# Three edits to the order of instructions: sums of tokens, first operands of the last stage, outputs of a pair

## The chip, the cores and the metric

The kernel runs on one core of a Trainium2 chip. The metric is the device time of one launch in microseconds (us); a kernel's time is the median of its runs. The engines are named as the profile names them: PE (matrix multiplications), DVE (vector engine), ACT (scalar engine), POOL (GpSimd), SP (SyncE, which issues most of the transfers). Each engine takes its instructions in the order in which they were issued to it.

## The reference

One input x of 2048 tokens by 576 features is normalised, and three things are added up: the input, a Fourier mixing of the normalised tokens, and a two-layer network on them.

```python
xn = layernorm(x)                                  # 2048 x 576
a, b = xn @ dft_hid_re.T, xn @ dft_hid_im.T        # transform along the features
y = dft_seq_re @ a - dft_seq_im @ b                # real part of the transform along the tokens
h = maximum(xn @ w1, 0)                            # 576 -> 4608
out = x + y + h @ w2                               # 4608 -> 576
```

All inputs are float32, and the four transform matrices are inputs like the others.

## The kernel before

**Arithmetic.** A float32 operand is split into two half-precision parts, hi and lo: ACT writes hi (a scaled copy that rounds), and DVE writes lo (the value minus hi). `split` (L182 on ACT, L183 on DVE) is the general form. A product takes three passes on PE: hi by lo, hi by hi, lo by hi. Larger products are cut into 2 by 2 blocks and done with seven block products in place of eight. The price is sums and differences of blocks on DVE and ACT; the names A11, S1 to S4, T1 to T4 and P1 to P7 are those blocks, block sums and products.

**Stages.** The tokens lie in four groups g of 512.

1. Normalisation of the first group, then the network in nine blocks b of 512 hidden units, each for four groups: a step is one pair (b, g). In a step PE computes the hidden values of (b, g) and the second product of the step before (`mlp2`, L510: seven products; evictions on ACT at L519 and on DVE at L521, from block 1 on added to a spill in main memory by POOL's queue). In blocks 0 and 1 the hidden values come from plain products of 512 columns (`mlp1_step`, L310; outputs in `mlp1_out`, L353 to L361, the last two being hi on ACT and lo on DVE of the four sums S1 to S4). While block 0 runs, the tokens of the following groups are still being normalised, and their weights loaded, scaled and split.
2. From block 2 on, the hidden values come from `pair_products` (L440; seven products on half the columns). They need sums of tokens as right-hand operands: `sums_x` makes four per group, 16 in all, with 56 DVE operations (L405, L406, L408, L409 and lo at L414) and 16 copies on ACT (L412). They are stored in the memory in which block 0's accumulators lay, once these have been written out, and use two temporaries in the weight buffers of block 1. They are handed out as small steps from an iterator `tq` between the products of block 1 and, as far as any are left, of block 2.
3. `dft1`: the transform along the features, for 16 tiles t of 128 tokens (PE at L1002). Outputs R[t]: a copy on ACT (L1022), sums on DVE (L1024 to L1027), hi on ACT (L1030) and lo on DVE (L1031) of three blocks, and at the end hi (L1033) and lo (L1034) of the four sums T.
4. The last stage: 16 units, each with seven products of 24 matmuls (L1116) that sum over 8 tiles R. The left-hand operand of each is made from a unit's four loads `c` by `operand` (L1055 to L1071: sums on DVE at L1063, L1064, L1066 and L1068 where the product needs them, then `split`) into a ring `cs` of four buffers, three products ahead. Evictions are on DVE (L1122). The first three operands are made before the stage begins: their steps come from a list `todo`, one step after each tile of `dft1` from t = 2 on. Ahead of the three stand the scale of the operands, the loads of the first unit, and empty steps, so that the three are called after tiles 13, 14 and 15.

**What sets the order.** The program's calls are only a draft. A planner with its own estimates of times sorts the instructions, and may move one ahead of others on its engine where no dependence forbids it. `tc.issue_after(ins)` forbids it: what is issued inside it stays behind `ins` if it is on the same engine; no wait is added. `order["s"]` is the latest hi of the four sums on ACT (L360, and L459 in `pair_products`), `order["lo"]` the latest lo on DVE (L361, L462).

**A pair's list.** In a step of block 2 and after, two `pair_products` (`first`, `second`) are woven with the step's seven second products (`m`), with small steps of the weights' preparation (`ready`), with passes over the transform matrices (`count`), and with the hi and lo of the sums (`end`). `first(q)` issues a product with what frees its bank; `later1(q)` and `later2(q)` issue what makes outputs of it. The order is a list of pairs (L919 to L927 of the kernel before).

Of the kernel before, what the change touches and what calls it, by code (L numbers as in the profile page):

```python
# [13 lines left out]
AF = mybir.ActivationFunctionType  # L14
ALU = mybir.AluOpType
# [34 lines left out]
def kernel(  # L50
# [17 lines left out]
    nc = tc.nc  # L68
# [119 lines left out]
    means, factors, shifts, order = {}, {}, {}, {}  # L188
# [190 lines left out]
    def halves(g, q):  # L379

        r, c = q
        k, t = 2 * r, (H1, H2)[c]
        return xT[g][:, k : k + 2, t], xT[g][:, KM + 1 + k : KM + 3 + k, t]
# [7 lines left out]
    def sums_x(g):  # L391


        f = [
            w[:, 2 * KT * P :][:, : 2 * GH].rearrange("p (k t) -> p k t", t=GH) for w in w1bufs[2:]
        ]
        tt = nc.vector.tensor_tensor
        for q, (head, tail) in enumerate((
            ((0, 1), (0, 0)), ((1, 1), None), ((1, 0), None), ((1, 1), (0, 1)),
        )):  # L400
            t = f[q % 2]
            h, l = halves(g, head)
            if tail:
                h2, l2 = halves(g, tail)
                tt(t, h, h2, ALU.subtract)  # L405
                tt(t, t, l2, ALU.subtract)  # L406
            else:
                tt(t, h, f[1 - q % 2], ALU.subtract)  # L408
            tt(t, t, l, ALU.add)  # L409
            yield  # L410
            hi, lo = (xsums[g][:, q, n] for n in range(2))
            nc.scalar.activation(hi, t, AF.Copy)  # L412
            yield
            tt(lo, t, hi, ALU.subtract)  # L414

    banks1, ends = [], []

# [464 lines left out]
    for n in range(2, len(steps)):  # L882
        b, g = steps[n]
        pb, pg = steps[n - 1]
        if g == 0 and b:
            if b + 1 < NB:
                todo += prepare_block(b + 1)
            else:
                todo += [lambda: (load_d(0), load_d(1)), lambda: None, new_d, lambda: None]
                for j in range(4):  # L890
                    d = power_d(j)
                    todo += [lambda d=d: next(d), lambda d=d, j=j: (later(d), split_d(j))]
                    if j < 2:
                        todo += [lambda j=j: load_d(j + 2), lambda: None]
                todo += [scales_d]
        if b == 0 and g + 1 < NG:
            with tc.issue_after(order["lo"]):
                weave(stats([(g + 1) * TG + i for i in range(TG)]))
        if b == NB - 1 and g:

            size = 2 * EH
            if g == 1:
                w = mlp.tile([P, 2, 7, EH], F16, tag="w2s", name="sums", bufs=4)
                w = [w.rearrange("p n q e -> p (n q e)").bitcast(F32)]
            elif g == 2:
                w = [raw.tile([P, KT, EH], F32, tag="raw", name=f"sums{k}") for k in range(2)]
                w = [r.rearrange("p k e -> p (k e)") for r in w]
            sumbufs[:] = [
                r[:, k : k + size].rearrange("p (c e) -> p c e", e=EH)
                for r in w for k in range(0, r.shape[1] - size + 1, size)  # L910
            ]
        if b >= BB:
            first, second = (pair_products(b, g, i) for i in range(NQ))
            later1, later2 = (lambda q, f=f: f(q, True) for f in (first, second))
            m = lambda q: mlp2(pb, pg, q)
            end = lambda q: ends and ends.pop(0)()
            ready = lambda q: [work() for _ in range(q)]
            count = lambda q: n > 3 and passes and passes.pop(0)()
            for do, q in (  # L919
                (first, P1), (first, P2), (m, 0), (end, 0), (first, P6), (ready, 1),  # L920
                (first, P5), (later1, P2), (ready, 1), (m, 1), (end, 0), (second, P1), (ready, 1),
                (first, P7), (m, 2), (second, P2), (later1, P7), (ready, 1),
                (first, P3), (first, P4), (count, 0), (later1, P3), (m, 3), (later1, P4), (second, P6),
                (later2, P2), (ready, 1), (m, 4), (end, 0), (second, P5), (ready, 1), (m, 5), (end, 0),
                (second, P7), (ready, 1), (m, 6), (ready, 2), (second, P3), (later2, P7),
                (count, 0), (second, P4), (later2, P3), (later2, P4), (ready, 1),
            ):  # L927
                do(q)
            for _ in range(4):
                next(tq, None)  # L930
            continue
        ps = []
        for i in range(NF):
            if n == 2:
                ps.append(early.pop(0) if early else mlp1(b, g, i))
            else:
                mlp1_step(b, g, i, ps)
            if i % 2:
                mlp1_out(b, g, i // 2, *ps[i - 1 : i + 1])
            if b == 0 and g + 1 < NG:  # L940
                t = (g + 1) * TG + i
                normalize(t)
                remainder(t, nc.gpsimd)
                transposes(t)
            if n == 2 and i == 2:
                todo += prepare_block(1)
            for _ in range(1 if b else 3):
                work()
            for q in range(2 * i, min(2 * i + 2, 7)):
                mlp2(pb, pg, q)  # L950
                if b:
                    next(tq, None)
            if b and i == 3:
                next(tq, None)
            for _ in range(1 + i % 2 if b else 3):
                work()
            if n > 3 and i % 2 and passes:
                passes.pop(0)()
# [30 lines left out]
    def dft1(t):  # L989
# [40 lines left out]
            nc.scalar.activation(hi, src, AF.Copy, scale=r)  # L1030
            stt(lo, src, r, hi, ALU.mult, ALU.subtract)  # L1031
        hi, lo = (R[t][:, n, T3 : T2 + 1] for n in range(2))
        nc.scalar.activation(hi, T, AF.Copy)  # L1033
        nc.vector.tensor_tensor(lo, T, hi, ALU.subtract)  # L1034

    A = {}

# [18 lines left out]
    def operand(m):  # L1056

        n, i = divmod(m, 7)
        q = PRODUCTS[i][0]
        a11, a22, a12, a21 = (A[n, j] for j in range(4))  # L1060
        tt = nc.vector.tensor_tensor
        if q == S2:
            tt(a21, a21, a22, ALU.add)  # L1063
            tt(a11, a21, a11, ALU.subtract)  # L1064
        elif q == S3:
            tt(a21, a22, a11, ALU.subtract)  # L1066
        elif q == S4:
            tt(a12, a12, a11, ALU.subtract)  # L1068
        src = {A11: a11, A22: a22, A12: a12, S1: a21, S2: a11, S3: a21, S4: a12}[q]
        w = csp[m] = cs.tile([P, 2, HK, P], F16, tag="cs", name=f"cs{m}")  # L1070
        split(w[:, 0], w[:, 1], src, sc["c"][:, n : n + 1])  # L1071

    todo += [power_c, lambda: None, lambda: load_c(0)] + [lambda: None] * 8
    todo += [lambda m=m: operand(m) for m in range(3)]
    for t in range(NT):
        if t and t % TG == 0:
            xpool[t // TG - 1].release()
# [104 lines left out]
```

## Time and profile before

| what | value |
|---|---|
| median of 3 runs | 1283.66 us (1282.51 to 1285.61) |
| the profiled execution | 1285.6 us, of which its span is 1283.8 |
| PE busy | 1247.0 us, 97% of the span |
| DVE busy | 1002.9 us, 78% |
| ACT busy | 727.8 us, 57% |
| POOL busy | 149.0 us, 12% |
| moved | 150.75 MB |

Times in the profile count from the start of the span. A row of a timeline gives the start, the length, the engine, the line, the operation, output<-inputs with their shapes, the number of instructions drawn together, and in brackets the idle time of the engine ahead of it and what ended that. A group has the count, busy time, mean of one in ns, and the idle time ahead of its members with the releasers. Matmuls overlap, so a row of n matmuls lasts a little longer than n times their distance.

Block 0 ends near 138 us (the last lo of its hidden values), block 1 runs to about 217, where PE's first L440 matmuls stand between those of L510, and block 2's first pair has its lo at 233. `dft1` runs from 830, where its first matmuls stand between the last of L510, to 949, and the last stage from there to the end.

### The profile page before, as it was taken

How to read it: one execution, taken by the hardware profiler on the slowest of the kernel's cores; microseconds unless marked ns; L12 is line 12 of the kernel's file. 1: busy time of each engine (PE TensorE's matmuls, PEld its weight loads, DVE VectorE, ACT ScalarE, POOL GpSimd, SP SyncE). 2: the span in 40 equal slices, each digit the busy share in tenths (PEclk: the TensorE clock that was granted, in tenths of full speed). 3: DMA queues.
4: the chain of work that ended last, by engine and by line, in shares of the span. 5: the costliest groups of instructions: out<-in, count | busy, mean ns of one | idle time of the engine just before them, and what ended most of it. 6: DMA issues, size and time to landing. Idle time of an engine off the chain costs nothing.

```text
span 1283.8 us, 25483 instructions
## 1 busy us (share of the span) xinstructions
PE 1247.0 (97%) x10396; PEld 990.4 (77%) x10396; DVE 1002.9 (78%) x1879; ACT 727.8 (57%) x1218; POOL 149.0 (12%) x188
## 2 busy tenths in 40 slices
PE   7899999999999999999999999999999999999998
PEld 7665566888888888878878887867777777777776
DVE  8989998786877776777867877567668788888875
ACT  5835567676776676766766765544443333333332
POOL 2320012111112121211121111100000000000000
PEclk9899999999999999999999999999999999999999
DMA  6112457566756675666666665630033435344320
GB/s 242 43 62 69 124 124 153 131 116 142 146 131 122 133 149 121 133 136 126 120 142 143 138 135 121 111 94 17 1 124 113 153 105 165 117 127 135 127 85 20
DMA packets 60806, 150.75 MB, mean 117 GB/s; under 512 B 6288, under 2 KB 21136, under 8 KB 60688
## 3 DMA queue, kind: packets, MB, share of 16 engines
q1 hardware_dynamic: 42256, 111.36, 27.1%
q0 software_dynamic: 18432, 37.76, 20.9%
q8 instruction: 81, 1.33, 0.4%
q14 instruction: 37, 0.30, 0.1%
HBM read 101.91 MB, written 47.19 MB: 116 GB/s over the span
## 4 chain that ended last, share of the span: by engine, by line
PE 69%; DVE 17%; ACT 5%; DMA 5%; issue 3%; SPq 1%; POOL 0%; ACTq 0%; POOLq 0%; DVEq 0%
PE p L1116 25%; PE p L510 17%; PE bank L440 17%; PE pd L1002 7%; DMA raw_w<-in_w_dram 2%; DVE w2s L183 2%; PE p L310 2%; ACT h L459 1%; DVE h L448 1%; DVE h L462 1%; ACT f L874 1%; DMA c<-in_cim_dram 1%; DMA c<-in_cre_dram 1%; DVE dbuf L183 1%; DVE w1buf L183 1%
## 5 line engine op out<-in xcount | busy, mean ns | idle before, releaser
L510 PE MATMUL p<-w2s,h 128*128 128x288 f16 x3024 | 409.8, 286 | 4.7 <-DVE acc L521 2.0
L510 PEld LDWEIGHTS <-h 128*128 128x128 f16 x3024 | 295.0, 98 | 81.3 <-issue 6.1
L1116 PE MATMUL p<-R,cs 128*128 128x288 f16 x2688 | 329.6, 286 | 1.8 <-DVE o L1122 1.8
L1116 PEld LDWEIGHTS <-cs 128*128 128x128 f16 x2688 | 263.0, 98 | 68.2 <-issue 2.0
L182 ACT ACTIVATE cs<-c,sc_c 128x1024 f16<-128x1024 f32 x112 | 128.5, 1148 | 205.1 <-PE p L1116 151.3
L183 DVE SCALAR_TENSOR_TENSOR cs<-c,sc_c,cs 128x1024 f16<-128x1024 f32 x112 | 143.7, 1283 | 50.9 <-ACT cs L182 50.8
L440 PEld LDWEIGHTS <-w1buf 128*128 128x128 f16 x1600 | 156.4, 98 | 30.4 <-issue 9.3
L440 PEld LDWEIGHTS <-dbuf 128*128 128x128 f16 x1200 | 117.3, 98 | 22.7 <-issue 7.0
L440 PE MATMUL bank<-xT,w1buf 128*128 128x256 f16 x832 | 109.8, 273 | 1.9 <-ACT acc L469 1.9
L1002 PE MATMUL pd<-dbuf,xT 128*128 128x288 f16 x832 | 106.0, 289 | 2.4 <-DVE R L1031 2.4
L440 PE MATMUL bank<-acc,w1buf 128*128 128x256 f16 x768 | 102.1, 272 | 4.6 <-DVE acc L470 2.9
L462 DVE TENSOR_TENSOR h<-s,h 128x1024 f16<-128x1024 f32 x56 | 68.5, 1224 | 48.4 <-ACT h L459 48.4
L1002 PEld LDWEIGHTS <-xT 128*128 128x128 f16 x832 | 81.5, 99 | 25.8 <-issue 4.8
L523 POOL DMA_DIRECT2D spill<-dbuf x74 | 64.1, 868 | 291.9 <-DVE dbuf L521 225.8
L440 PE MATMUL bank<-xT,dbuf 128*128 128x256 f16 x624 | 82.3, 273 | 1.6 <-ACT acc L469 1.6
L447 ACT ACTIVATE h<-acc 128x256 f16<-128x256 f32 x112 | 46.3, 414 | 59.9 <-DVE acc L470 43.6
L440 PE MATMUL bank<-acc,dbuf 128*128 128x256 f16 x576 | 76.6, 272 | 3.1 <-ACT s L468 1.7
L448 DVE SCALAR_TENSOR_TENSOR h<-acc,h 128x256 f16<-128x256 f32 x112 | 47.3, 423 | 35.1 <-ACT h L447 34.8
L1122 DVE SCALAR_TENSOR_TENSOR o<-p,us_c,o 128x288 f32<-128x288 f32 x112 | 57.5, 514 | 20.3 <-PE p L1116 20.3
L459 ACT ACTIVATE h<-s 128x1024 f16<-128x1024 f32 x56 | 59.0, 1053 | 20.9 <-DVE s L454 19.6
L874 ACT ACTIVATE f<-f 128x1024 f32<-128x1024 f32 x64 | 67.1, 1049 | 5.1 <-DMA f<-in_cre_dram 5.1
L519 ACT ACTIVATE dbuf<-p,c_ub 128x576 f32<-128x576 f32 x74 | 54.1, 732 | 21.4 <-ACT h L447 11.3
(158 smaller groups left out, 1538.7 us busy)
## 6 DMA issues: line engine op xcount, KB each, us to landing
spill<-dbuf POOLq DMA_DIRECT2D x74, 288.0 KB, 5.2
f<-in_cre_dram SPq DMA_DIRECT2D x32, 512.0 KB, 4.5
f<-in_cim_dram SPq DMA_DIRECT2D x32, 512.0 KB, 3.7
c<-in_cre_dram SPq DMA_DIRECT2D x32, 512.0 KB, 4.6
c<-in_cim_dram SPq DMA_DIRECT2D x32, 512.0 KB, 4.8
spill<-sum POOLq DMA_DIRECT2D x38, 288.0 KB, 5.2
raw_w<-in_w_dram SPq DMA_DIRECT2D x17, 640.0 KB, 5.0
raw_w<-in_w_dram SPq DMA_DIRECT2D x18, 576.0 KB, 3.8
```

What stands on the lines that cost most here:

```text
L182: nc.scalar.activation(hi, src, AF.Copy, scale=s)
L183: nc.vector.scalar_tensor_tensor(lo, src, s, hi, ALU.mult, ALU.subtract)
L440: nc.tensor.matmul(ps, l, r, start=first and m == 0, stop=m == len(todo) - 1, skip_group_check=not first,)
L448: stt(lo, src, 0.0, hi, ALU.max, ALU.subtract)
L459: order["s"] = nc.scalar.activation(hi_s, st[:, 1:], AF.Copy).ins
L462: order["lo"] = nc.vector.tensor_tensor(lo_s, st[:, 1:], hi_s, ALU.subtract).ins
L510: nc.tensor.matmul(ps[:, c], h[:, x, qa, c * P : (c + 1) * P], w[:, y, qb], start=first and i == 0 and j == 0, stop=i == NQ - 1 and j == 2 ...
L523: nc.gpsimd.dma_start(spill[g, row, col], o, accum_op=ALU.add)
L874: nc.scalar.activation(f, f, AF.Abs, scale=2.0**-10, accum_out=sums_c[:, n, q : q + 1])
L1002: nc.tensor.matmul(ps[j], xT[g][:, kx, c * P : (c + 1) * P], dsp[j][:, hl, k], start=(t % 2 == 0 and n == 0), stop=(t % 2 == 1 and n == le ...
L1116: nc.tensor.matmul(ps, w[:, a, k], r[:, c, rq], start=first and k == 0 and j == 0, stop=k == HK - 1 and j == 2, skip_group_check=not first,)
L1122: nc.vector.scalar_tensor_tensor(o, ps, us["c"][:, n : n + 1], o, ALU.mult, ALU.add)
```

## The change

1. In `sums_x`, the DVE operations are issued behind `order["lo"]` and the copy behind `order["s"]`, as they are at the moment of the call: behind the latest hidden values' lo and hi.
2. In `dft1`, `order["lo"]` and `order["s"]` are set to the lo and hi of T, and the first three operands of the last stage are issued behind them on DVE and ACT. The three calls come after tiles 13, 14 and 15.
3. In the list of a pair's step, the outputs of P7, P3 and P4 of the first product, some of the sums' hi and lo, and the outputs of P7 of the second, come later.

```diff
@@ -400,18 +400,21 @@
         )):
             t = f[q % 2]
             h, l = halves(g, head)
-            if tail:
-                h2, l2 = halves(g, tail)
-                tt(t, h, h2, ALU.subtract)
-                tt(t, t, l2, ALU.subtract)
-            else:
-                tt(t, h, f[1 - q % 2], ALU.subtract)
-            tt(t, t, l, ALU.add)
+            with tc.issue_after(order["lo"]):
+                if tail:
+                    h2, l2 = halves(g, tail)
+                    tt(t, h, h2, ALU.subtract)
+                    tt(t, t, l2, ALU.subtract)
+                else:
+                    tt(t, h, f[1 - q % 2], ALU.subtract)
+                tt(t, t, l, ALU.add)
             yield
             hi, lo = (xsums[g][:, q, n] for n in range(2))
-            nc.scalar.activation(hi, t, AF.Copy)
+            with tc.issue_after(order["s"]):
+                nc.scalar.activation(hi, t, AF.Copy)
             yield
-            tt(lo, t, hi, ALU.subtract)
+            with tc.issue_after(order["lo"]):
+                tt(lo, t, hi, ALU.subtract)
 
     banks1, ends = [], []
 
@@ -919,11 +922,11 @@
             for do, q in (
                 (first, P1), (first, P2), (m, 0), (end, 0), (first, P6), (ready, 1),
                 (first, P5), (later1, P2), (ready, 1), (m, 1), (end, 0), (second, P1), (ready, 1),
-                (first, P7), (m, 2), (second, P2), (later1, P7), (ready, 1),
-                (first, P3), (first, P4), (count, 0), (later1, P3), (m, 3), (later1, P4), (second, P6),
-                (later2, P2), (ready, 1), (m, 4), (end, 0), (second, P5), (ready, 1), (m, 5), (end, 0),
-                (second, P7), (ready, 1), (m, 6), (ready, 2), (second, P3), (later2, P7),
-                (count, 0), (second, P4), (later2, P3), (later2, P4), (ready, 1),
+                (first, P7), (m, 2), (second, P2), (ready, 1), (first, P3), (first, P4), (count, 0),
+                (later1, P7), (m, 3), (second, P6), (later1, P3), (later1, P4), (later2, P2),
+                (ready, 1), (m, 4), (second, P5), (ready, 1), (m, 5), (end, 0), (second, P7),
+                (end, 0), (ready, 1), (m, 6), (count, 0), (ready, 2), (second, P3), (second, P4),
+                (later2, P7), (later2, P3), (later2, P4), (ready, 1),
             ):
                 do(q)
             for _ in range(4):
@@ -1030,8 +1033,8 @@
             nc.scalar.activation(hi, src, AF.Copy, scale=r)
             stt(lo, src, r, hi, ALU.mult, ALU.subtract)
         hi, lo = (R[t][:, n, T3 : T2 + 1] for n in range(2))
-        nc.scalar.activation(hi, T, AF.Copy)
-        nc.vector.tensor_tensor(lo, T, hi, ALU.subtract)
+        order["s"] = nc.scalar.activation(hi, T, AF.Copy).ins
+        order["lo"] = nc.vector.tensor_tensor(lo, T, hi, ALU.subtract).ins
 
     A = {}
 
@@ -1071,7 +1074,11 @@
         split(w[:, 0], w[:, 1], src, sc["c"][:, n : n + 1])
 
     todo += [power_c, lambda: None, lambda: load_c(0)] + [lambda: None] * 8
-    todo += [lambda m=m: operand(m) for m in range(3)]
+    def first_operand(m):
+        with tc.issue_after(order["s"]), tc.issue_after(order["lo"]):
+            operand(m)
+
+    todo += [lambda m=m: first_operand(m) for m in range(3)]
     for t in range(NT):
         if t and t % TG == 0:
             xpool[t // TG - 1].release()
```

## The prediction

> **What bounds the kernel now.** I read the page's busy shares and groups first, then the windows by stage, then the idle time in TensorE's (PE's) timeline with its releasers, because PE turns out to be the bound.
>
> ```profile
> span 1283.8 us, 25483 instructions
> PE 1247.0 (97%) x10396; PEld 990.4 (77%) x10396; DVE 1002.9 (78%) x1879; ACT 727.8 (57%) x1218; POOL 149.0 (12%) x188
> L1116 PE MATMUL p<-R,cs 128*128 128x288 f16 x2688 | 329.6, 286 | 1.8 <-DVE o L1122 1.8
> ```
>
> PE is idle for 1283.8 − 1247.0 = 36.8 us in all, and the whole last stage (L1116) holds one wait of 1.8. So a gap that vanishes anywhere earlier shortens the run by its length, and a new one at the last stage's start lengthens it by its length.
>
> ```profile
> core 0: us, PE busy (x) PEld busy (x) DVE busy (x) ACT busy (x) POOL busy (x), PEclk, DMA share, GB/s
> 60.00:138.40 78.40, 72.70 (x486) 43.95 (x484) 69.94 (x142) 36.09 (x59) 7.27 (x9) 1.00 0.26 88
> 138.40:233.30 94.90, 94.12 (x641) 61.38 (x639) 84.52 (x167) 62.33 (x109) 13.70 (x17) 1.00 0.55 122
> ```
>
> Columns: window, length, busy time of each engine. Block 0 (60 to 138.4) holds 5.7 us of PE's idle time while the vector engine (DVE) is 89% busy; block 1 (to 233.3, where block 2's first h is complete) holds 0.8. This is measured on one execution of 1285.6 us (span 1283.8 and 1.8 around it), 1.9 above the median of the runs, 1283.66. I sum changes and apply them to both.
>
> **The pair order (third edit).** It changes the order of calls; a planner decides the order of instructions. In the built kernels, the DVE, PE and scalar engine (ACT) streams of blocks 2 to 7 are the same, instruction by instruction. I cost it at nothing there, with no cover needed. The streams differ in blocks 0 and 1, at one place in block 8, and around the first transform.
>
> **Sums held back, what leaves block 0.** These are the sums that DVE makes there now:
>
> ```profile
> L409 DVE TENSOR_TENSOR dbuf<-dbuf,xT 128x512 f32<-128x512 f32 x5 | 3.9, 784 | 0.0
> L414 DVE TENSOR_TENSOR acc<-dbuf,acc 128x512 f16<-128x512 f32 x5 | 3.4, 679 | 0.7 <-DMA spill<-acc 0.7
> L406 DVE TENSOR_TENSOR dbuf<-dbuf,xT 128x512 f32<-128x512 f32 x3 | 2.3, 754 | 0.0
> L405 DVE TENSOR_TENSOR dbuf<-xT 128x512 f32<-128x512 f16 x3 | 2.1, 709 | 0.3 <-POOL dbuf L250 0.3
> L408 DVE TENSOR_TENSOR dbuf<-xT,dbuf 128x512 f32<-128x512 f16 x2 | 1.4, 692 | 0.9 <-PE pt L263 0.9
> ```
>
> That is 18 operations, 3.9 + 3.4 + 2.3 + 2.1 + 1.4 = 13.1 us. In the built order all 18 and their ACT copies go behind block 0's last h. PE's waits in block 0 that have a sum ahead of their releaser, and one DVE row:
>
> ```profile
> 81.01 3.10 PE L510 MATMUL p<-w2s,h 128*128 128x288 f16 x24 [0.58 <-DVE acc L521]
> 84.72 1.14 PE L510 MATMUL p<-w2s,h 128*128 128x288 f16 x8 [0.62 <-DVE acc L521]
> 100.99 2.97 PE L310 MATMUL p<-xT,w1buf 128*128 128x512 f16 x13 [1.17 <-ACT xT L265]
> 117.00 0.27 PE L158 MATMUL pm<-ident,mb 128*1 128x128 bf16 x2 [0.40 <-DVE mb L614]
> 137.15 0.42 PE L510 MATMUL p<-w2s,h 128*128 128x288 f16 x2 [0.86 <-ACT h L360]
> ```
>
> ```profile
> 83.25 0.69 DVE L414 TENSOR_TENSOR acc<-dbuf,acc 128x512 f16<-128x512 f32 x1 [0.71 <-DMA spill<-acc]
> ```
>
> The rows add to 0.58 + 0.62 + 1.17 + 0.40 + 0.86 = 3.6. The second wait is plain: DVE itself stood 0.71 in a sum's store, which waits until the spilled accumulator has been written out, with PE's eviction (L521) behind it. The others are queueing: the xT copy waits on ACT behind a weight split whose scale DVE makes late. The last two can have a weight load beneath them and may stay, and buffers freed earlier may only let PE reach the next load sooner: I take −3.4, between −1.2 (the two evictions alone) and −5.3 (nearly all of the 5.7).
>
> **What they cost in block 1.** DVE has to fit them in by block 2:
>
> ```profile
> 140.00:200.00 60.00, 60.00 (x384) 36.37 (x383) 59.45 (x118) 37.47 (x62) 8.26 (x10) 1.00 0.51 110
> 220.00:233.30 13.30, 13.30 (x118) 11.24 (x116) 6.56 (x15) 8.17 (x19) 0.86 (x1) 1.00 0.54 121
> ```
>
> ```profile
> 177.99 0.81 DVE L521 SCALAR_TENSOR_TENSOR dbuf<-p,c_ub,dbuf 128x576 f32<-128x576 f32 x1
> 180.25 3.10 PE L510 MATMUL p<-w2s,h 128*128 128x288 f16 x24
> 204.81 1.63 PE L510 MATMUL p<-w2s,h 128*128 128x288 f16 x12 [0.78 <-DVE dbuf L521]
> ```
>
> Of 94.9 us DVE is busy 84.5, and adding the 13.1 gives 97.6 (by starts of instructions, which overlap a little at the ends, 82.8 + 12.3 = 95.1). From 140 to 200 DVE idles 0.55 us in 60, so it needs almost no idle time when its queue is full; the slack, 6.7 us, lies after 220. The extra work there therefore starts late by 7 us less the 2.5 to 3 that DVE gains from block 0's gaps. PE does not follow one for one: the eviction at 177.99 ends at 178.8 and its next matmul is the thirteenth of the 24 from 180.25, at 181.6 (2.8 spare), and in the new order 5 to 13 plain matmuls go ahead of the waiting ones (row at 100.99: 2.97 / 13 = 0.22 each, 1.1 to 2.9). But the eviction before 204.81 has no spare, PE already waits 0.78 for it. I take +1.5, from 0 (all covered) to +7.6 (the slower rival). Nothing is gained: PE's idle time here is that 0.78. The sums' ACT copies (16, beside 62 of 94.9 us busy) are covered. The SyncE queue takes one w2 load a place earlier, ahead of a spill, and GpSimd moves one reduction four spills on; both move by single places and no wait on them ends last here: 0.
>
> **Block 8.** One addition (L470) moves ahead of a 1.72 us split:
>
> ```profile
> 781.55 1.72 DVE L183 SCALAR_TENSOR_TENSOR dbuf<-raw_d,c_sd,dbuf 128x1440 f16<-128x1440 f32 x1
> 783.18 0.42 DVE L470 TENSOR_TENSOR acc<-bank,acc 128x256 f32<-128x256 f32 x1
> 783.66 0.82 PE L440 MATMUL bank<-acc,w1buf 128*128 128x256 f16 x6 [1.36 <-DVE acc L470]
> ```
>
> 1.72 is more than the wait: −1.4 (0 if the split then holds up the next eviction, −1.4 at most).
>
> **First operands held back, the start of the first transform.** Now two operand splits sit among the first tiles' evictions and wait for their loads:
>
> ```profile
> 844.40 1.15 ACT L182 ACTIVATE cs<-c,sc_c 128x1024 f16<-128x1024 f32 x1 [5.89 <-DMA c<-in_cre_dram]
> 848.75 1.15 ACT L182 ACTIVATE cs<-c,sc_c 128x1024 f16<-128x1024 f32 x1 [2.81 <-DMA c<-in_cim_dram]
> ```
>
> ```profile
> 850.89 0.28 PE L1002 MATMUL pd<-dbuf,xT 128*128 128x288 f16 x1 [0.45 <-DVE R L1031]
> 851.74 0.28 PE L1002 MATMUL pd<-dbuf,xT 128*128 128x288 f16 x1 [0.57 <-DVE R L1031]
> 853.36 6.86 PE L1002 MATMUL pd<-dbuf,xT 128*128 128x288 f16 x41 [1.34 <-DVE R L1031]
> ```
>
> ```profile
> 851.10:854.50 3.40, 1.49 (x12) 1.01 (x11) 3.40 (x6) 1.94 (x3) 0.00 (x0) 1.00 0.00 0
> 854.50:857.90 3.40, 3.40 (x17) 2.17 (x15) 3.37 (x6) 0.90 (x1) 0.00 (x0) 0.50 0.00 0
> 963.70:967.10 3.40, 1.70 (x14) 1.36 (x14) 3.37 (x4) 1.11 (x1) 0.00 (x0) 1.00 0.42 170
> ```
>
> ACT's evictions of R stand behind a split for 5.89 and 2.81 us, and PE then waits 0.45 + 0.57 + 1.34 = 2.36. After a window in which PE was busy 1.49 of 3.40, the granted clock (eighth column) is 0.50 for one window: another 3.40 × 0.5 = 1.7. After the last row's window, 1.70 of 3.40, it was not (row at 965.40 below: 29.81 / 242 = 0.123 a matmul, full pace). With the splits behind tiles 13 and 14, both costs go: −4.1 (−2.4 to −4.5; the queue then meets only evictions, which keep pace from 860 on).
> The Trainium skill, page "TensorE: Matmul & The Clock Gate", section "HAM oscillation — how this bites in real kernels", gives the rule as "no PE-idle gaps >~3.4µs"; by it these gaps would be free of it. The trace differs: single gaps of at most 1.34 us, 2.36 together, brought a half-clock window.
>
> **The same operands, the start of the last stage.** The third operand (S2) needs two additions and a split, and all three now stand behind R15's last lo (L1034).
>
> ```profile
> 948.76 14.86 PE L1116 MATMUL p<-R,cs 128*128 128x288 f16 x120
> 965.40 29.81 PE L1116 MATMUL p<-R,cs 128*128 128x288 f16 x242 [1.77 <-DVE o L1122]
> ```
>
> ```profile
> 953.15 1.36 DVE L1034 TENSOR_TENSOR R<-T,R 128x1152 f16<-128x1152 f32 x1 [0.30 <-ACT R L1033]
> 963.70 1.23 DVE L1063 TENSOR_TENSOR c<-c,c 128x1024 f32<-128x1024 f32 x1 [3.45 <-DMA c<-in_cre_dram]
> ```
>
> ```profile
> L182 ACT ACTIVATE cs<-c,sc_c 128x1024 f16<-128x1024 f32 x112 | 128.5, 1148 | 205.1 <-PE p L1116 151.3
> L183 DVE SCALAR_TENSOR_TENSOR cs<-c,sc_c,cs 128x1024 f16<-128x1024 f32 x112 | 143.7, 1283 | 50.9 <-ACT cs L182 50.8
> L1122 DVE SCALAR_TENSOR_TENSOR o<-p,us_c,o 128x288 f32<-128x288 f32 x112 | 57.5, 514 | 20.3 <-PE p L1116 20.3
> ```
>
> In before's clock: products 0 and 1 are 48 matmuls from 948.76 at 14.86 / 120 = 0.124, to 954.7. R15's lo lets DVE go at 954.4; L1063 1.2, one eviction 0.4 (0.51 less the overlap of the next), L1064 1.2: 957.2. ACT makes hi in 1.15 to 958.4, DVE lo in 1.28 to 959.7. PE idles 954.7 to 958.4 = 3.8, does two matmuls of product 2 and two of product 3 (whose hi ends near 959.6) in the built order, and waits 0.9 more for lo: +4.7. The gap spans parts of two 3.4 us windows, and one of them will be under half busy in nearly any phase: +1.7. Against that, the wait of 1.77 at 965.40 goes, since DVE's stop for unit 1's loads (3.45) then lies beside PE's new gap, and unit 2's first load, now ahead of eight reloads of outputs on SyncE's queue, moves behind unit 1's: −1.8. Net +4.6, from +2.9 (no slow window) to +6.4 (the 1.77 stays). Queued behind the held additions on DVE are the evictions of products 0 and 1; PE needs their banks only four products on.
>
> **Sum.** −3.4 + 1.5 − 1.4 − 4.1 + 4.6 = −2.8, beside −0.4 of small waits of block 0 (each under 0.25) that go with the sums: −3.2. The profiled execution would take 1285.6 − 3.2 = 1282.4 and the median 1283.66 − 3.2 = 1280.4. A change of 0.2%, 2.57 us, is about what a measurement of this kernel can tell: faster is below 1281.1, slower above 1286.2.
>
> **Rivals.**
> Slower: DVE becomes the bound in block 1. If its 10.4 us of idle time there are waits that come back whatever is queued (in order: for ACT's hi, for a product), all 12.3 us of added work come on top; less the lead of 2.7 and 2.0 of plain matmuls ahead PE gets 7.6 instead of 1.5: −3.2 + 6.1 = +2.9, 1286.6. It decides from 7.3 in block 1. The 0.55 idle in 60 us speaks against it, the eviction without spare at 204.81 for it.
> No change: block 0's waits turn into waits for weights that arrive when they did, and only the two evictions' 1.2 is gained: −3.2 + 2.6 = −0.6, 1283.1. For it: the waits at 117.00 and 137.15 lie next to weight steps. Against: the two evictions and the xT copy have no load of weights beneath them.
> Faster: no slow window at the transition, −3.2 − 1.7 = −4.9, 1278.8; by the row at 963.70 it takes a window half busy, with 3.8 us of gap split evenly over two.
> By the skill's rule above the gap would have to fill a whole 3.4 us window, and 3.8 us seldom does; it would give this same rival's 1278.8.
> That the third edit changes blocks 2 to 7 after all: no, the order there is the same.
>
> **Chances.** The forecast 0.42, from 1278.6 to 1282.4, two thirds of it under 1281.1 (0.27 faster, 0.15 same); the faster rival 0.18; no change 0.20; slower 0.20. Together 0.45, 0.35, 0.20. The range goes from 1276.9 (the faster rival with block 0's gain at 5.3 and the first transform's at 4.5) to 1287.0 (the slower rival and 0.4).
>
> **What the new profile would show.** Block 0: no L405 to L414 before 137, PE's idle time there under 2.5 us, its last h lo some 3 to 4 us earlier. Block 1: DVE near 99% until the first pair of block 2, PE's waits on L521 around 200 to 233 of 1 to 3 us in all; 7 or more proves the slower rival. 783: no wait. 845 to 858: no wait, PEclk 1.00. The last stage: PE waits about 3.8 and 0.9 behind `cs` at product 2, one window at 0.50 after it, and no wait of 1.77. The prediction fails if block 1's overrun passes 7, if block 0's gaps only change their releaser, or if the planner's order runs otherwise because loads land at other times.

## The result and the profile after

The changed kernel takes 1288.01 us (median of 13 runs, 1284.96 to 1290.39) against 1283.69 for the kernel before, run beside it: a ratio of 1.0027, 95% interval 1.0014 to 1.0039. It is slower by about 3.5 us by the ratio (the two medians differ by 4.3), where 1280.4, faster, was forecast; the range ended at 1287.0. The profiled execution took 1289.39 us (span 1287.6), 1.4 above the median.

The page of the changed kernel (its lines stand three to seven below those of the kernel before: L513 was L510, L1123 was L1116):

```profile
span 1287.6 us, 25468 instructions
PE 1247.5 (97%) x10396; PEld 990.2 (77%) x10396; DVE 1003.7 (78%) x1879; ACT 727.5 (56%) x1218; POOL 147.3 (11%) x188
L513 PE MATMUL p<-w2s,h 128*128 128x288 f16 x3024 | 409.9, 286 | 9.2 <-DVE dbuf L524 2.6
L1123 PE MATMUL p<-R,cs 128*128 128x288 f16 x2688 | 332.2, 288 | 4.0 <-ACT cs L182 4.0
```

The work is the same; the second products (L513) wait 9.2 us and not 4.7, and the last stage (L1123) 4.0 and not 1.8. Where the time went is read from PE's order: each kernel issues 10396 matmuls, and the start of the n-th in one profile less its start in the profile of before gives how far PE is ahead or behind at that place. Worked out from the traces (negative is ahead):

| n | place | before, us | changed | sums alone (e1) | 10 moved (e11) | 18 moved (e12) |
|---|---|---|---|---|---|---|
| 1000 | block 0 | 123.1 | −3.2 | −4.7 | −3.6 | −4.2 |
| 1100 | start of block 1 | 140.5 | −3.9 | −5.4 | −4.6 | −4.9 |
| 1550 | end of block 1 | 211.9 | +1.6 | −0.5 | −4.1 | +1.3 |
| 2000 | block 2 | 265.2 | +5.3 | +1.7 | −2.9 | +6.0 |
| 6340 | block 8, before the edit's place | 779.9 | +4.1 | −0.4 | −3.0 | +3.5 |
| 6400 | block 8, after it | 788.2 | +2.6 | −0.4 | −4.5 | +2.0 |
| 7000 | first transform | 863.7 | −1.1 | +0.8 | −8.2 | −1.3 |
| 7780 | start of the last stage | 957.6 | +5.7 | +0.8 | −8.2 | −1.3 |
| 10000 | last stage | 1231.5 | +3.8 | +2.9 | −5.7 | −1.5 |

Such columns come from one execution each; kernels with the same order in a stretch differ there by 1 to 3 us (from 2000 to 6340, where nothing was changed, the columns read −1.2, −2.1, −0.1 and −2.5). They are also measured from one execution of before: four other kernels with before's order of sums (e2, e3, e4 and e14 below) read −0.8 to −1.4 at n = 1100. The medians below carry the verdicts.

**What went as forecast.** Block 0 gave 3.2 to 3.9 in this profile. Over all profiles, the eight with no sum left in block 0 read −5.0 at n = 1100 in the mean and those four with before's order −1.2, which puts the gain at 3.9. The wait of 1.36 in block 8 is gone. The first transform's start gave 4.0: one wait of 0.34 is left, and no window at half clock. The last stage's start cost +6.8, less 1.9 for the wait that went: +4.9. PE's waits there, and the window that follows (its last columns are the granted clock, the DMA share and GB/s):

```profile
853.96 6.16 PE L1005 MATMUL pd<-dbuf,xT 128*128 128x288 f16 x49 [0.34 <-DVE R L1034]
...
957.37 0.66 PE L1123 MATMUL p<-R,cs 128*128 128x288 f16 x2 [3.64 <-ACT cs L182]
958.41 7.77 PE L1123 MATMUL p<-R,cs 128*128 128x288 f16 x44 [0.38 <-ACT cs L182]
```

```profile
955.90:962.40 6.50, 4.65 (x19) 2.65 (x20) 5.87 (x6) 3.38 (x4) 0.00 (x0) 0.52 0.62 219
```

**What did not.** Between n = 1100 and 2000 PE loses 9.2 us, where 1.5 was forecast. The loss has two parts: 5.5 until 1550, in evictions of block 1, and 3.8 at the entry of block 2. PE's waits in these two, of the changed kernel:

```profile
139.12 3.10 PE L513 MATMUL p<-w2s,h 128*128 128x288 f16 x24 [0.88 <-DVE acc L524]
159.87 1.63 PE L513 MATMUL p<-w2s,h 128*128 128x288 f16 x12 [1.32 <-DVE sum L524]
183.48 1.63 PE L513 MATMUL p<-w2s,h 128*128 128x288 f16 x12 [1.29 <-DVE dbuf L524]
209.31 4.45 PE L513 MATMUL p<-w2s,h 128*128 128x288 f16 x35 [1.26 <-DVE dbuf L524]
236.58 1.63 PE L513 MATMUL p<-w2s,h 128*128 128x288 f16 x12 [1.76 <-ACT dbuf L522]
```

The first four are evictions on DVE, 4.75 us together. DVE is not simply full there:

```profile
60.00:138.40 78.40, 75.18 (x502) 46.00 (x502) 63.37 (x132) 34.79 (x56) 6.73 (x10) 1.00 0.28 94
140.00:200.00 60.00, 57.23 (x365) 34.36 (x362) 56.85 (x114) 36.40 (x62) 7.58 (x9) 1.00 0.50 109
200.00:220.00 20.00, 18.50 (x122) 11.55 (x119) 19.82 (x35) 13.77 (x25) 3.00 (x4) 1.00 0.47 111
```

From 140 to 200 it is busy 56.85 us, less than the 59.45 of before, while more work stands in its queue. Of the 3.15 us of idle time, 1.80 (1.70 in e1, which has the same order) belong to one loop through ACT. The sum's copy (L414) waits on ACT for a sum that DVE makes late; hi of the hidden values (L360) stands behind it and behind a pass over newly loaded weights (L607); and DVE's lo (L361), with the evictions behind it, waits for that hi. Before the DVE row of this loop stands the eviction that PE's wait at 183.48 is for:

```profile
184.06 0.63 ACT L414 ACTIVATE acc<-dbuf 128x512 f16<-128x512 f32 x1 [2.17 <-DVE dbuf L410]
185.36 1.16 ACT L607 ACTIVATE j<-raw_w 128x1152 f32<-128x1152 f32 x1 [0.67 <-DMA raw_w<-in_w_dram]
```

```profile
182.61 0.81 DVE L524 SCALAR_TENSOR_TENSOR dbuf<-p,c_ub,dbuf 128x576 f32<-128x576 f32 x1
...
188.22 1.23 DVE L361 TENSOR_TENSOR h<-s,h 128x1024 f16<-128x1024 f32 x1 [1.80 <-ACT h L360]
```

The second part, at the entry of block 2, begins at a buffer. The last split of block 2's second weights on DVE frees the buffer for block 3's weights. It ended at 209.9 in before and at 223.4 in the changed kernel, so the load on SyncE's queue went out 13 us later, and ACT stood 1.60 us for it. ACT then stood 2.34 for the next block of the transform matrices (f), and DVE and PE behind it. First two rows of the timelines of before, then rows of the changed kernel's (SPq marks what SyncE issues):

```profile
208.38 1.55 DVE L183 SCALAR_TENSOR_TENSOR w2s<-raw_w,c_sw,w2s 128x576 f16<-128x576 f32 x2
...
224.83 1.06 ACT L874 ACTIVATE f<-f 128x1024 f32<-128x1024 f32 x1 [2.70 <-DMA f<-in_cre_dram]
```

```profile
222.61 0.81 DVE L183 SCALAR_TENSOR_TENSOR w2s<-raw_w,c_sw,w2s 128x576 f16<-128x576 f32 x1
...
223.44 0.33 SPq L107 DMA_DIRECT2D raw_w<-in_w_dram  x1
...
226.56 0.33 SPq L870 DMA_DIRECT2D f<-in_cre_dram  x1
...
228.71 1.27 ACT L581 ACTIVATE dbuf<-raw_w 128x1280 f16<-128x1280 f32 x1 [1.60 <-DMA raw_w<-in_w_dram]
233.35 1.06 ACT L877 ACTIVATE f<-f 128x1024 f32<-128x1024 f32 x1 [2.34 <-DMA f<-in_cre_dram]
...
235.36 0.43 DVE L454 SCALAR_TENSOR_TENSOR s<-acc,s 128x256 f32<-128x256 f32 x1 [3.89 <-ACT s L479]
```

The load of f did not go out 13 us late: it left at 226.56, as soon as ACT's own pass before it had ended at 226.5, and before has a wait of 2.70 for the same load, which cost PE nothing. So how much of the 3.8 us is the late weights' load, and how much DVE's and ACT's lateness alone, is not told by this profile.

### The profile page after: what moved, and what is told of

Its sections match the earlier page's. It is cut to its first block, busy times and chain, and to the rows that moved or that the text cites. A ratio compares the mean times of both kernels' runs of the same rounds, so it can differ in the third digit from the quotient of the medians.

```text
span 1287.6 us, 25468 instructions
## 1 busy us (share of the span) xinstructions
PE 1247.5 (97%) x10396; PEld 990.2 (77%) x10396; DVE 1003.7 (78%) x1879; ACT 727.5 (56%) x1218; POOL 147.3 (11%) x188
## 4 chain that ended last, share of the span: by engine, by line
PE 61%; DVE 19%; DMA 8%; ACT 7%; issue 4%; POOL 1%; SPq 0%; ACTq 0%; POOLq 0%; DVEq 0%
PE p L1123 25%; PE bank L443 14%; PE p L513 14%; PE pd L1005 7%; DMA raw_w<-in_w_dram 4%; DVE w2s L183 2%; DMA f<-in_cre_dram 1%; DMA spill<-dbuf 1%; PE p L310 1%; DVE h L451 1%; DVE h L465 1%; ACT h L462 1%; DVE dbuf L183 1%; ACT f L877 1%; DVE acc L524 1%
## 5 line engine op out<-in xcount | busy, mean ns | idle before, releaser
L513 PE MATMUL p<-w2s,h 128*128 128x288 f16 x3024 | 409.9, 286 | 9.2 <-DVE dbuf L524 2.6
L513 PEld LDWEIGHTS <-h 128*128 128x128 f16 x3024 | 294.9, 98 | 86.4 <-issue 11.8
L1123 PE MATMUL p<-R,cs 128*128 128x288 f16 x2688 | 332.2, 288 | 4.0 <-ACT cs L182 4.0
L1123 PEld LDWEIGHTS <-cs 128*128 128x128 f16 x2688 | 263.8, 98 | 72.3 <-ACT cs L182 4.8
```

What stands on the lines that cost most here:

```text
L513: nc.tensor.matmul(ps[:, c], h[:, x, qa, c * P : (c + 1) * P], w[:, y, qb], start=first and i == 0 and j == 0, stop=i == NQ - 1 and j == 2 ...
L1123: nc.tensor.matmul(ps, w[:, a, k], r[:, c, rq], start=first and k == 0 and j == 0, stop=k == HK - 1 and j == 2, skip_group_check=not first,)
```

## The experiments

**Each edit alone.** In the built orders the three edits do not touch each other: each alone has the changed kernel's order at its own places and before's elsewhere, but for two neighbouring DVE instructions. The edits are those of the diff above.

> Only the first edit (sums of tokens held back behind block 0's hidden values); the built order is the changed kernel's up to block 7 and before's after it. Theory: the loss of the changed kernel is made in block 1, where in its profile PE's progress against before goes from -3.2 us (end of block 0) to +5.3 us (block 2), because DVE's queue keeps its idle time of 14.9 us (14.4 before) and the added sums come on top. Then this alone is slower: +4.5 to +6 us, about 1289. Rival: the loss is made at the start of the last stage by half-clock windows (its profile shows two there, and its runs fall in two groups 3.4 us apart); block 1 is then given back later and this is within 2 us of before, in one group.

> Only the second edit (first operands held back behind the first transform's outputs). Theory, from the changed kernel's profile: -4.0 at the start of the first transform, +4.9 at the start of the last stage, together +0.9 us (1284.6), in two groups of runs by whether one or two windows at half clock follow the gap there. Rival (half-clock windows carry the whole loss): +3 to +4 us, 1287.

> Only the third edit (the list of a pair's step). The built order differs from before at one place alone, in block 8, where an addition comes ahead of a split. Theory: the wait of 1.36 us at 783 goes, -1.4 us, 1282.3. Rival: the split then holds up an eviction instead, 0.

| run | median, us | ratio to before, 95% interval |
|---|---|---|
| e1, sums | 1287.80 | 1.0023 (1.0009 to 1.0036) |
| e2, operands | 1284.42 | 1.0002 (0.9989 to 1.0015) |
| e3, pair order | 1283.60 | 0.9991 (0.9978 to 1.0003) |

The whole loss is the first edit's: about +3 us, where +4.5 to +6 was expected. The second comes out at zero, a gain and a loss of nearly the same size (4.0 and 3.8 in its profile, and the loss with one window at half clock, not two); the third's 1.2 us is as forecast but lies within its interval. The rival that put the loss on the half-clock windows of the last stage falls: e2, which has the gap, is not slower.

**The operands held back earlier.** Four empty steps in place of eight put the three operands behind tiles 9, 10 and 11:

```diff
-    todo += [power_c, lambda: None, lambda: load_c(0)] + [lambda: None] * 8
+    todo += [power_c, lambda: None, lambda: load_c(0)] + [lambda: None] * 4
```

(with the second and third edits, and the sums as in before)

> The second and third edits, with four empty steps in place of eight ahead of the three operands, so that they are held behind tiles 9, 10 and 11 of the first transform and not 13, 14 and 15; the sums are as in before. Theory: the gain at the start of the first transform stays (-4.0), the gap at the start of the last stage does not arise (0, or the 1.8 of before stays), block 8 gives -1.4: about -5.4 us, 1278.3. Rival: the splits among the tiles' evictions hold up PE there as they did at the start, and the gain is lost: 1282 to 1284.

It took 1278.32, ratio 0.9951 (0.9933 to 0.9970): −6.2 us, where −5.4 was expected. The gain at the first transform's start stays (4.3 in its profile) and no gap opens at the last stage's. So the gap was the price of the place behind the last tiles, not of holding the operands back. Of the wait of 1.77 at the stage's start a longer one was left in its profile, as in before an eviction behind a sum that waits for unit 1's loads:

```profile
956.56 18.66 PE L1120 MATMUL p<-R,cs 128*128 128x288 f16 x151 [2.59 <-DVE o L1126]
```

**Is it DVE's amount of work in block 1?** In e5 the sums of group 0 are left out:

```diff
             h, l = halves(g, head)
+            if g == 0:
+                yield
+                with tc.issue_after(order["s"]):
+                    for n, src in enumerate((h, l)):
+                        nc.scalar.activation(xsums[g][:, q, n], src, AF.Copy)
+                yield
+                continue
```

> The changed kernel, with the four sums of group 0 left out (14 of the 56 DVE operations of the sums, some 10 us; ACT copies two halves of the tokens in their place, so the values that the pairs of group 0 use are not the sums). They are nearly the 18 operations that the first edit moves from block 0 to block 1. Theory: the loss in block 1 is DVE's added work behind waits that stay; with it left out block 0's gain stays alone, PE enters block 2 at -3 against before instead of +5.3, and the kernel takes about 1280. Rival: the loss is made by loads of weights and of the transform matrices that the new order issues later (ACT waits 2 to 3 us for some in block 1); then it stays, 1286 or more.

It took 1287.31, 1.0024 (1.0013 to 1.0034): nothing was gained, and the theory in this form fell. The time is the rival's, but the profile (of an execution of 1283.04, the fastest of its 11) shows no late load as its cause. In it PE keeps its lead up to n = 1350 (−4.7, where the changed kernel has −0.8), and loses most of it in one wait, behind an eviction ahead of which the planner had now put sums of block 2's weights (L644 to L647):

```profile
203.14 0.45 DVE L647 TENSOR_TENSOR raw_w<-raw_w 128x288 f32<-128x288 f32 x1
203.51 0.68 DVE L417 TENSOR_TENSOR dbuf<-dbuf,xT 128x512 f32<-128x512 f32 x1
204.11 0.81 DVE L531 SCALAR_TENSOR_TENSOR dbuf<-p,c_ub,dbuf 128x576 f32<-128x576 f32 x1
```

```profile
204.97 1.36 PE L520 MATMUL p<-w2s,h 128*128 128x288 f16 x5 [3.32 <-DVE dbuf L531]
```

The planner put other work where the sums had been, so leaving them out does not measure their price here.

**The sums' last step on GpSimd.**

```diff
-            with tc.issue_after(order["lo"]):
-                tt(lo, t, hi, ALU.subtract)
+            nc.gpsimd.tensor_tensor(lo, t, hi, ALU.subtract)
```

> The changed kernel, with the sums' last step (lo, 16 operations of 0.69 us, 11 us) on GpSimd in place of DVE. Theory (DVE's work is the price): block 1's 8.5 shrink to about 1, total near 1281. Rival: GpSimd takes 1.2 to 1.6 us for such a step, and its queue also issues the spills, which come late; no gain, 1287 or more.

> As the one before (lo of the sums on GpSimd, all sums held back), and with the operands held behind tiles 9 to 11 as in the run e4. Theory: the two add up: 1281 - 5.5 = 1275.5. Rival: as for the run before, 1281 or more.

The first took 1297.90, 1.0108 (1.0092 to 1.0123), the second 1290.99, 1.0066 (1.0048 to 1.0085): the rival was right. The step takes 1.37 us on GpSimd (0.69 on DVE) and stands among the spills that GpSimd issues. In e6's profile an eviction on ACT waits for a spill to free its buffer, and PE for that eviction:

```profile
207.26 0.74 ACT L521 ACTIVATE dbuf<-p,c_ub 128x576 f32<-128x576 f32 x1 [2.79 <-DMA spill<-dbuf]
```

```profile
208.05 5.23 PE L512 MATMUL p<-w2s,h 128*128 128x288 f16 x24 [5.08 <-ACT dbuf L521]
```

**Fewer sums held back, and the weights ahead.** In e8 the sums are held behind one fixed place, the hidden values of block 0, group 2, with the operands as in e4. In the built order 8 of the 18 operations stay in block 0, and 10 move. Part of the edit (the copy on ACT is held behind `order["s2"]` in the same way):

```diff
+        if (b, g) == (0, 2):
+            order["s2"], order["lo2"] = order["s"], order["lo"]
...
-            with tc.issue_after(order["lo"]):
+            with tc.issue_after(order["lo2"]):
```

> All three edits with the operands behind tiles 9 to 11, and the sums held back only behind the hidden values of (block 0, group 2), not of group 3, so that some run in block 0's second half. Theory: the two waits behind sums at 81 and 84 and the one at 99.8 still go (about -2), and block 1 gets about half of the 13 us: +2 to +3; 1278 to 1279, no better than the run e4 (1278.3). Rival (what block 1 loses depends on the last few operations alone): 1275 to 1276.

e8 took 1282.13, 0.9988 (0.9979 to 0.9997), 3.8 above e4. In its profile 10 moved operations cost little in block 1 (−4.0 at n = 1100, −3.4 at 1550). The loss is one stall at the entry of block 2, where ACT waits for block 3's weights:

```profile
219.10 1.27 ACT L583 ACTIVATE dbuf<-raw_w 128x1280 f16<-128x1280 f32 x1 [4.95 <-DMA raw_w<-in_w_dram]
```

```profile
223.92 1.44 PE L445 MATMUL bank<-acc,w1buf 128*128 128x256 f16 x6 [4.19 <-ACT s L473]
```

and after it a stretch at half clock:

```profile
223.90:229.70 5.80, 5.78 (x26) 3.78 (x26) 1.82 (x4) 3.12 (x7) 0.88 (x1) 0.50 0.77 173
```

So the next runs move the last split of the weights ahead, by one more step of the preparation in each turn of the last step of block 1, once in the changed kernel (e9), once in e8 (e11), and once with all sums behind block 0's last hidden values (e12; e10 is e12 without the weights' step; both have `(b, g) == (0, 3)` in the edit of e8):

```diff
-            for _ in range(1 + i % 2 if b else 3):
+            for _ in range(1 + i % 2 + (g == 3) if b else 3):
                 work()
```

> The changed kernel, with one more step of the weights' preparation called per turn in the last step of block 1 (b = 1, g = 3). In the built order the last split of block 2's second weights (w2s, L183 on DVE) then stands ahead of the last three sums of tokens in place of between them (place 409 in DVE's order, 424 in the changed kernel, 418 in before). Theory now: the loss at the entry of block 2 comes from this split: it frees the buffer for block 3's weights, whose second load was issued at 210 in before and at 223.4 in the changed kernel, and ACT then stands in order for that load. With the split ahead, the 3.8 us of that place go: 1284 to 1285. Rival: DVE's lateness alone counts, 1287 or more.

> All three edits with the operands behind tiles 9 to 11, and all sums held back behind one fixed place, the last hidden values of block 0, where the changed kernel holds each behind the hidden values last called before it, so that in block 1 every step's sums also wait for that step's own lo. As many DVE operations move to block 1 as in the changed kernel. Theory: the waits of evictions in block 1 (5.5 us from 138 to 212) come from the hold within block 1, so PE keeps most of its -3.9 up to the last step of block 1; the stall at the entry of block 2 by the weights stays (last split at place 424): 1281 to 1283. Rival (the number of operations in block 1 counts): PE loses 5 us by 212, total 1283 to 1284, as the changed kernel less 5.5.

> The run e8 (sums held behind block 0, group 2; operands early) with the weights' preparation called one step more per turn in the last step of block 1; the last split then stands at place 414 and not 421. Theory: e8's stall of 4.19 us at 219.7 behind ACT's wait for block 3's weights, and the two windows at half clock after it, go or shrink: 1282.1 less 4 to 7, 1275 to 1278. Rival: 1281 or more.

> The run e10 (all sums behind the last hidden values of block 0) with the weights' preparation called one step more per turn in the last step of block 1: last split at place 414 and not 424. Theory: 1276 to 1279, 4 or more below e10. Rival (DVE's work in block 1 counts): no better than e10.

| run | operations moved | last split's place in DVE's order | median, us | ratio, 95% interval |
|---|---|---|---|---|
| changed kernel | 18, behind each step's own lo | 424 | 1288.01 | 1.0027 (1.0014 to 1.0039) |
| e9 | the same | 409 | 1286.89 | 1.0013 (1.0003 to 1.0022) |
| e10, operands early | 18, fixed place | 424 | 1281.58 | 0.9973 (0.9957 to 0.9988) |
| e12, operands early | 18, fixed place | 414 | 1284.60 | 1.0000 (0.9989 to 1.0011) |
| e8, operands early | 10 | 421 | 1282.13 | 0.9988 (0.9979 to 0.9997) |
| e11, operands early | 10 | 414 | 1275.73 | 0.9932 (0.9915 to 0.9948) |

e11 shows the route over the buffer most plainly. The load of block 3's weights went out at 208.2 and not at 212.8, and the stall of e8 is gone: −6.4 us between the medians, 7 by the ratios, where 4 to 7 was expected. Its rows at the same places (of its slowest execution; e13 below, the same kernel, shows waits of 0.64 and 0.17 there):

```profile
213.65 1.27 ACT L583 ACTIVATE dbuf<-raw_w 128x1280 f16<-128x1280 f32 x1 [1.08 <-DMA raw_w<-in_w_dram]
```

```profile
215.97 1.47 PE L445 MATMUL bank<-acc,w1buf 128*128 128x256 f16 x12 [0.60 <-ACT acc L471]
```

It does not carry over to every kernel. e9 gained less than expected (its interval meets the changed kernel's); in its profile the load went out at 212.8, ACT's wait for it is gone, and PE still loses 2.8 us at the entry of block 2, with a wait of 1.60 for f left. And e12 is 3.0 slower than e10, against the theory. In e12's profile ACT waits for another transfer at that place (2.35 us for a spill) and PE stands 2.90 with a half-clock window behind it; so which transfer lands late at the entry of block 2 differs from order to order, and this part stays open beyond e8 and e11, for the changed kernel too.

e10's time is the one expected, but its profile refutes the idea behind it, that holding the sums behind each step's own hidden values makes the first part of the loss: with one fixed place and the same 18 operations PE loses 5.8 by n = 1550 (−5.6 to +0.2), as much as the changed kernel.

**The dose.** Three runs side by side: 10 moved again, none moved again, 15 moved (held behind the first pair of hidden values of block 0, group 3, `(b, g, i) == (0, 3, 0)` in the edit of e8; otherwise as e11).

> The run e11 again (10 of the 18 sum operations moved out of block 0, weights' preparation ahead, operands early), beside the two that follow on one chip. If its lead over e4 is real, it stays 1.5 us or more below e14: 1275 to 1277. If it is chance, they are equal.

> The run e4 again (none of the 18 operations moved, operands early): 1278 to 1279.

> As e13, with the sums held behind the first pair of hidden values of (block 0, group 3): 15 of the 18 operations move, 3 stay in block 0. Dose theory (DVE in block 1 has some 7 to 8 us to spare, and what goes beyond it is paid by PE nearly one for one): 15 x 0.73 = 11 us moved, 3 to 4 us beyond it, 1279 to 1281, between e11 (10 moved, 0.5 us lost by the end of block 1 in its profile) and e12 (18 moved, 6.1 lost, 1284.6). Rival (the number does not matter, another place in the order does): equal to e11 or to e12.

| operations moved, operands early | run | median, us | ratio, 95% interval | PE's loss from n = 1100 to 1550, us |
|---|---|---|---|---|
| 0 | e14 | 1278.19 | 0.9949 (0.9937 to 0.9962) | 0.0 |
| 10 | e13 | 1277.17 | 0.9935 (0.9921 to 0.9948) | 0.6 |
| 15 | e15 | 1281.05 | 0.9966 (0.9954 to 0.9979) | 4.7 |
| 18 | e12 | 1284.60 | 1.0000 (0.9989 to 1.0011) | 6.1 |

What PE loses up to n = 1550 rises with the number. Ten operations, 10 × 0.73 = 7 us, find room in block 1; the next five and three cost PE 4.1 and 1.4. The other profiles agree: 0.6 in e8 and 0.5 in e11 with 10 moved; 5.5 in the changed kernel, 4.9 in e1, 5.0 in e9 and 5.8 in e10 with 18. The number is not parted from the order that comes with it: each dose has its own place of hold, the row with none lacks the step that moves the weights ahead, the run of e12 is not one of the three side by side, and 2.89 of e15's 4.7 us are one wait, behind an eviction ahead of which eight sums of block 2's weights stand (the same eviction costs 1.09 in e13, 2.89 in e10 and e12). That wait is where e5, with fewer sums, lost as much.

The kernel with ten moved (e11, e13) is the fastest made here, 8 to 9 us under before. Against none moved its lead is 1.0 us, where 1.5 or more was expected, with intervals that meet, so what the sums give when held back in part is not settled; what the early operands and the pair order give is.

## Why the prediction was wrong

**Block 0 (−3.4 and −0.4): right.** PE was 3.2 to 3.9 ahead at its end, in e1 4.7 to 5.4; between the means of the profiles with all moved and none moved lie 3.9.

**Block 1 (+1.5, from 0 to +7.6): this step failed.** From n = 1100 to 2000 the changed kernel lost 9.2. Three things in it were wrong.

First, PE's lead was booked as a gain in block 0 and its evictions' spare time was booked again in block 1. An eviction's spare is counted in before's clock; a PE that is ahead uses it up. The eviction at 177.99 had 2.8 us of spare and was taken as covered. In the changed kernel it stands at 182.61 and ends 4.6 later, about the lateness that was forecast (7 less 2.5 to 3); five more matmuls stood ahead of the waiting ones, as forecast, but PE came 0.8 early, and waited 1.29 (4.6 − 2.8 − 5 × 0.22 + 0.8 = 1.5). The same was paid at three other evictions (0.88, 1.32 and 1.26), of which the working had looked at one. The 6.7 us of slack after 220 was no help, since these evictions come before 212. The dose shows about what there was: room for 7 us, and beyond it PE paid for 8 operations, 5.8 us of work, with 5.5.

Second, DVE's idle time came back. The rival "slower" said that the waits return whatever is queued, priced it at 7.6, and gave 1286.6 for the kernel; it was the nearer account. The forecast that DVE would be near 99% busy until block 2's first pair failed: 56.85 of 60 us, or 95%, from 140 to 200. More than half of the idle time there is the loop through ACT: the sums' copies, costed as covered because ACT was busy 62 of 94.9 us, stand ahead of hi in ACT's queue.

Third, SyncE's queue was costed at 0, since its loads moved "by single places". Counted in places the step was nothing, counted in time the load of block 3's weights went out 13 us later, because what frees its buffer had moved on DVE. No rival named the entry of block 2. There the changed kernel lost 3.8. In e8, which lost 7.2 there, moving that split ahead removed the loss (e11); in the changed kernel it removed 1.0 in the profile (e9), so the rest of the 3.8 stays open.

**Pair order (0 in blocks 2 to 7) and block 8 (−1.4): right.** The place in block 8 gave 1.5 in the profiles, e3 −1.2 (from −2.8 to +0.4).

**Start of the first transform (−4.1): right,** 4.0 in the changed kernel.

**Start of the last stage (+4.6): right in sum, with two terms off that cancel.** The waits were 4.0 in place of 4.7, and half clock lasted two windows of 3.4 us in place of one. The wait of 1.77 went as said. That the sum came out at 4.9 is in part luck: the same waits brought one window in e2 and e9, and the start cost 3.8 and 4.4 there. Taken together the second edit was forecast at +0.5; e2 measured 0.3 (from −1.4 to +1.9).

Of the chances, "slower" had 0.20, the weight of one mechanism at its limit. The block's row of idle time, 0.8 us of PE in 94.9 with DVE at 89%, left nothing to gain and much to lose, and deserved more.

## What to carry to other kernels

When work moves onto an engine that is nearly full, compare it with the spare time of the tightest waiters in the stretch, one by one, take off what the waiting engine has gained before, and do not count the idle total of the stage; here about 7 us were free and the next 6 were paid nearly one for one. Follow each buffer that the delayed engine frees to the load that waits for it, and to the engine that stands in order for that load: a queue order that hardly changed can still send its transfer 13 us later. And before discarding an edit that gains and loses, look whether the gain and the loss hang on the same place: the operands held behind tile 9 and not 13 kept the 4 us and, in e4's profile, paid 0.8 in place of 4.9.

## What the runs showed of the hardware

The granted clock falls to a half in windows of 3.41 us that lie on a fixed grid. In each of the 17 profiles every change of the clock lies a whole number of 3.413 us after the first, to 0.003 us, with the grid at another place in each execution. Worked out from the traces, the clock of a window follows PE's busy share in the window before it. Of windows at full clock (before 1270 us), all 38 under 0.415 busy were followed by one at half clock, 6 of the 8 from 0.415 to 0.45, and none of the 6204 above. A window at half clock was followed by another in all ten cases under 0.815 busy, and in none from 0.87 on.

So one length of gap does different things, depending on where it lies: 2.89 us brought no window (e10, at 202.5; split over windows busy 0.60 and 0.53), 2.90 brought one (e12, at 224.4; a window busy 0.38). The 3.64 and 0.38 us at the last stage's start brought two in the changed kernel and one in e2. The changed kernel's windows first, then e2's; after the length come PE's busy time and further on the granted clock:

```profile
952.71:956.12 3.41, 1.02 (x9) 0.59 (x6) 3.41 (x4) 0.00 (x0) 0.00 (x0) 1.00 0.90 296
956.12:959.53 3.41, 1.78 (x7) 0.82 (x8) 3.38 (x4) 2.19 (x2) 0.00 (x0) 0.50 0.94 340
959.53:962.95 3.42, 3.42 (x17) 2.13 (x15) 2.75 (x3) 1.75 (x2) 0.00 (x0) 0.50 0.31 92
```

```profile
948.28:951.69 3.41, 0.00 (x0) 0.00 (x1) 3.38 (x5) 1.20 (x2) 0.00 (x0) 1.00 0.88 297
951.69:955.10 3.41, 3.03 (x12) 1.55 (x13) 3.38 (x4) 0.99 (x1) 0.00 (x0) 0.50 0.74 282
955.10:958.51 3.41, 3.41 (x29) 2.74 (x28) 2.31 (x4) 2.98 (x3) 0.00 (x0) 1.00 0.53 159
```

The Trainium skill, page "TensorE: Matmul & The Clock Gate", section "HAM oscillation — how this bites in real kernels", warns of idle gaps above about 3.4 us; the gaps of 2.90 us in e12 and 3.32 us in e5, and the short ones at 851 in before, were enough. The Trainium skill's free-running window (same page, section "What's actually happening") agrees with the grid that these traces show.

The same instructions at the start of the program had windows at half clock in one profile and none in another: 17.5 to 24.3 and 34.5 to 37.9 in the changed kernel, none from 7 to 854 in e1 and e2. Whether this is why runs of one kernel spread over 5 us (1284.96 to 1290.39) stays open. In the changed kernel the five runs with a mean clock of 0.993 took 1288.6 to 1290.4, and the four with 0.997 or 0.998 1285.0 to 1285.7; in e1 the runs at 0.993 took 1284.4, 1284.8 and 1289.4. Single profiles could not be compared to better than 2 us.
